# A decode kernel whose KV buffers also take the space set aside for GpSimd's transfer descriptors

## The chip, the core and the metric

The kernel runs on one core of one Trainium2 chip. The metric is the device time of one execution in microseconds. The core's engines are TensorE (PE; PEld is its weight load), VectorE (DVE), ScalarE (ACT), GpSimd (POOL) and SyncE (SP), which only issues transfers here. All weights and caches lie in the chip's memory (HBM) and come to on-chip memory (SBUF, 128 partitions) through 16 DMA engines; TensorE writes its results to PSUM, which has eight banks.

## The reference, cut to what matters

Two layers, each an attention block A and a feed-forward block B, with the same weights in both layers, for 4 tokens of 448 features, one new position each:

```
x = A_x                                   # 4 x 1 x 448
x = x + A(layernorm(x)); x = x + B(layernorm(x))
x = x + A(layernorm(x)); x = x + B(layernorm(x))

A(x): q = x @ wq                          # 448 -> 16 heads x 256
      k, v = the last 2048 positions of k_cache, v_cache   # 8 KV heads, two q heads share one
      p = softmax(q . k / 16);  o = p @ v;  return o @ wo  # 4096 -> 448
B(x): return (silu(x @ w_gate) * (x @ w_up)) @ w_down      # 448 -> 1792 -> 448
```

Everything is bf16. Each token has its own cache. One KV head of one token has 2048 x 256 values of K and as many of V: 1 MiB each. 4 tokens x 8 heads x 2 MiB are 64 MiB, and both layers read the same cache. So a layer that finds a K or V of the layer before still in SBUF needn't load it again.

## The kernel before, in words

**Units of work.** The work is cut into 64 heads (token, layer, KV head), written as three digits: 107 is token 1, layer 0, head 7; 113 is token 1, layer 1, head 3. PLAN (line 48) lists them in 54 groups of one head or two. For each head K and V come in two halves of 512 KiB. A buffer for one half is 128 x 2048 bf16; NPOOL = 27 of them lie in `kv`, and seven more (NWQ) hold wq until its last use, then seven late halves too.

**One group** (`group`, lines 916 to 1080) is a chain over the engines: two K transposes of 32 x 32 blocks on VectorE (L935), the masked query on GpSimd (L974), the scores on TensorE (`scores`, L969, 32 matmuls), row maxima on VectorE and TensorE (L982, L987, L990, L996), the exponential on ScalarE (L1000), a turn of the weights (L1013, L1022), sums (L1030, L1035), the V product (`pv`, L1044, 8 matmuls for each half of V), its reordering (L1059, L1061, L1067), division (L1057, L1077), and the output projection (`out_proj`, L1089 or L1097). PSUM has two banks for scores (S), three for products (Y), one that accumulates the output (A) and two for the projections and the FFN (Z, Z2).

Where the two halves of a K lie at most REACH = 15 buffers apart, `keys` (line 909) reads both with one matmul; else each score matmul becomes two of half the width.

**Between layers** each token has its own chain: residual, norm, FFN (`ffn_row`, or `ffn` for late tokens), norm, and the projection of the next query (`qproj`, lines 637 to 699). Only after it can the token's layer 1 start. Layer 0 of the next tokens is interleaved with it, so the order of the whole is: token 0 layer 0; token 1 layer 0 beside token 0 layer 1; and so on to token 3 layer 1. The first projection does all four tokens at once and needs all of wq.

**Kept heads.** KEEP_K and KEEP_V give, for each token, how many of its last heads of layer 0 keep their K or V in the buffers for layer 1. Before it is 5+5+4+5 = 19 K and 5+5+5+3 = 18 V, 37 MiB in all. A K that is kept is transposed once only. A buffer becomes free at the scores (K) or at the V product (V) of its last use.

**The order is written out.** Each engine runs its operations in the order of a list (SEQ_PE, SEQ_DVE, SEQ_ACT, SEQ_POOL, SEQ_SP), by the numbers in which `build` creates them. SEQ_SP is the order in which SyncE issues loads, and SLOTS gives the buffer for each. `schedule` adds to each load the wait for the operation that frees its buffer. SyncE issues in order: a load that waits holds up all behind it. In the lists "w" and "q" on TensorE are fills: matmuls with zero weights that add nothing to A (L1191, one matmul of 128 x 512; L1197, four of 32 x 512). `_fill` orders them against the operations of other engines that read or write A, by start times of `schedule`'s own estimate.

**Where things lie.** Tiles are allocated one after the other (lines 383 to 434). The first 16 KiB of each partition are kept by the language for descriptors of transfers that GpSimd issues (DynamicDMAScratch). This kernel issues its transfers from SyncE, and one small one from ScalarE.

Of the kernel before, what the change touches and what calls it, by code (L numbers as in the profile page):

```python
# [8 lines left out]
BF16 = mybir.dt.bfloat16  # L9
# [4 lines left out]
B = 4  # L14
# [11 lines left out]
NPOOL = 27  # L26
# [4 lines left out]
KEEP_K = (5, 5, 4, 5)  # L31
KEEP_V = (5, 5, 5, 3)
# [53 lines left out]
).split()  # L86
SEQ_DVE = (
# [23 lines left out]
).split()  # L111
# [1156 lines left out]
```

## Time and profile before

| what | us |
|---|---|
| median of 3 runs (lowest, highest) | 294.4 (293.93, 295.44) |
| span of the profiled execution, first to last instruction | 291.7 |
| busy: PE, DVE, POOL, ACT | 221.3, 197.4, 86.5, 66.1 |
| mean granted TensorE clock | 0.815 of full |
| bytes moved | 108.28 MB, 371 GB/s over the span |

The span is that of one execution with the profiler on; the runs' time includes what lies before and after it. The chain that ended last, followed back from the end, is 36% PE, 31% DMA, 12% waits of SyncE's queue and 12% DVE. "Place" means, below, the MB that stand ahead of a load in SEQ_SP: it is counted from the list (512 KiB for a half, 1 MiB for a piece of wq, 0.46 MB for a piece of wo, and so on), and is the same in any run.

### The profile page before, as it was taken

Reading aid. Unit: us, or ns where it says so; the run is one execution under the profiler, and the core shown is the slowest. Engines: PE = TensorE matmul, PEld = TensorE weight load, DVE = VectorE, ACT = ScalarE, POOL = GpSimd, SP = SyncE. Lnnn points to the kernel's source line nnn. Section 1 sums busy time; section 2 is a strip of 40 time slices with the busy share of each in tenths; the row PEclk is TensorE's granted clock in tenths of the full one; section 3 lists DMA queues with packets and bytes.
Section 4 is the critical chain, followed back from the end, with each engine's and each line's share of the span. In section 5 each row is a group of like instructions: output and inputs, shape, how many; then the busy total and the mean of one; then the engine's idle time right before and its main releaser. Section 6 shows DMA issues by size and latency. Waiting matters only on the chain.

```text
span 291.7 us, 10739 instructions
## 1 busy us (share of the span) xinstructions
PE 221.3 (76%) x4684; PEld 129.5 (44%) x4684; DVE 197.4 (68%) x609; ACT 66.1 (23%) x191; POOL 86.5 (30%) x230
## 2 busy tenths in 40 slices
PE   0467569686977697869688787797798667899775
PEld 0313136233433454546335454566364435645455
DVE  7547584427665997974968769677838777848541
ACT  0030002022214232322323233312312322033310
POOL 1541003111322233324323523340221331433522
PEclk9997977957689777886959559857759998799997
DMA  7999999999999999999999999999989999999800
GB/s 284 413 404 407 424 407 409 401 404 406 391 408 407 389 408 408 394 383 358 412 395 356 409 408 407 407 406 379 369 317 372 403 410 388 367 374 401 354 6 3
DMA packets 30782, 108.28 MB, mean 371 GB/s; under 512 B 3083, under 2 KB 7183, under 8 KB 29327
## 3 DMA queue, kind: packets, MB, share of 16 engines
q1 hardware_dynamic: 30727, 107.60, 94.3%
q8 instruction: 37, 0.61, 0.8%
q14 instruction: 10, 0.08, 0.1%
q10 hardware_dynamic: 8, 0.00, 0.0%
HBM read 107.58 MB, written 0.00 MB: 369 GB/s over the span
## 4 chain that ended last, share of the span: by engine, by line
PE 36%; DMA 31%; SPq 12%; DVE 12%; issue 5%; ACT 1%; POOL 1%
DMA half<-in_A_k_cache_dram 16%; DMA half<-in_A_v_cache_dram 15%; PE Y L1044 8%; PE S L969 8%; DVE half L935 7%; SPq L945 5%; SPq L550 5%; PE Z L773 3%; PE Z L665 2%; PE A L1097 2%; SPq L931 2%; PE Y L1013 2%; PE Z L813 2%; DVE oh L1061 1%; PE Y L1067 1%
## 5 line engine op out<-in xcount | busy, mean ns | idle before, releaser
L935 DVE STREAM_TRANSPOSE half<-half 128x1024 uint32<-128x1024 uint32 x90 | 110.0, 1232 | 14.9 <-DMA half<-in_A_k_cache_dram 14.4
L1044 PE MATMUL Y<-half,pT 128*4 128x256 bf16 (+1 forms) x1024 | 53.4, 319 | 11.8 <-DMA half<-in_A_v_cache_dram 8.8
L969 PE MATMUL S<-half,qe 128*8 128x128 bf16 (+1 forms) x1728 | 48.3, 261 | 10.6 <-DVE half L935 5.3
L1057 POOL TENSOR_TENSOR small<-small 128x2 f32<-128x2 f32 (+1 forms) x54 | 40.7, 758 | 51.6 <-DVE small L1035 44.9
L969 PEld LDWEIGHTS S<-half,qe 128*8 128x8 bf16 x1728 | 33.7, 95 | 19.3 <-DVE half L935 8.2
L974 POOL TENSOR_TENSOR qe<-qc,tiny 128x64 bf16<-128x64 bf16 x64 | 18.2, 292 | 79.9 <-PE S L969 66.3
L1000 ACT ACTIVATE praw<-S,small 104x128 bf16<-104x128 f32 (+1 forms) x54 | 20.8, 385 | 75.2 <-DVE small L996 65.7
L1061 DVE SCALAR_TENSOR_TENSOR oh<-oh,small,Y 128x256 bf16<-128x256 bf16 x54 | 25.3, 468 | 10.9 <-ACT oh L1059 10.4
L1059 ACT ACTIVATE oh<-Y 128x256 bf16<-128x256 f32 x54 | 20.6, 382 | 47.1 <-PE Y L1044 32.2
L1044 PEld LDWEIGHTS Y<-half,pT 128*4 128x4 bf16 (+1 forms) x1024 | 19.4, 88 | 24.0 <-DMA half<-in_A_v_cache_dram 12.0
L982 DVE TENSOR_REDUCE tiny<-S 104x1 bf16<-104x128 f32 (+1 forms) x54 | 16.4, 306 | 11.7 <-PE S L969 11.4
L1022 ACT ACTIVATE pT<-Y 128x64 bf16<-128x64 f32 (+1 forms) x54 | 13.1, 242 | 44.0 <-PE Y L1013 36.7
L1097 PE MATMUL A<-wo_sb,oT 128*4 128x448 bf16 x168 | 17.1, 399 | 3.7 <-DVE oT L1077 2.2
L1191 PE MATMUL A<-identb,small 128*128 128x512 bf16 x54 | 19.4, 444 | 0.0
L996 DVE TENSOR_REDUCE small<-S 104x1 f32<-104x32 f32 x54 | 9.6, 181 | 10.8 <-PE S L990 6.8
L665 PE MATMUL Z<-half,xn 128*5 128x512 bf16 x160 | 15.1, 530 | 1.6 <-DVE st L601 1.3
L1035 DVE TENSOR_REDUCE small<-Y 128x2 f32<-128x32 f32 (+1 forms) x54 | 10.0, 186 | 9.2 <-PE Y L1030 8.2
L987 PE MATMUL S<-small,identb 104*104 104x32 bf16 x54 | 12.5, 234 | 4.3 <-DVE tiny L982 3.3
L1077 DVE TENSOR_TENSOR oT<-Y,small 128x4 bf16<-128x4 f32 (+1 forms) x62 | 9.1, 157 | 7.8 <-PE Y L1067 4.4
L990 PE MATMUL S<-identb,tiny 104*104 104x32 bf16 x54 | 11.6, 219 | 3.6 <-issue 3.6
L1013 PE MATMUL Y<-sel,praw 104*64 104x32 bf16 x176 | 11.4, 206 | 3.7 <-ACT praw L1000 2.4
L1067 PE MATMUL Y<-tiny,oh 128*128 128x2 bf16 (+1 forms) x108 | 10.9, 171 | 3.8 <-DVE oh L1061 3.4
(142 smaller groups left out, 252.2 us busy)
## 6 DMA issues: line engine op xcount, KB each, us to landing
half<-in_A_v_cache_dram SPq DMA_DIRECT2D x92, 512.0 KB, 7.8
half<-in_A_k_cache_dram SPq DMA_DIRECT2D x74, 512.0 KB, 7.7
half<-in_A_k_cache_dram SPq DMA_DIRECT2D x8, 1024.0 KB, 16.4
wo_sb<-in_A_wo_dram SPq DMA_DIRECT2D x8, 448.0 KB, 14.9
half<-in_A_wq_dram SPq DMA_DIRECT2D x3, 1024.0 KB, 6.5
wd_sb<-in_B_w_down_dram SPq DMA_DIRECT2D x1, 1568.0 KB, 20.4
wg_sb<-in_B_w_gate_dram SPq DMA_DIRECT2D x1, 1344.0 KB, 16.8
wu_sb<-in_B_w_up_dram SPq DMA_DIRECT2D x1, 1344.0 KB, 17.3
```

What stands on the lines that cost most here:

```text
L665: last = e.matmul(zb[32 * j:32 * j + B + 1, 0:512], lhsT=lhsT, rhs=wq_sb[:, c:c + 512], start=(cc == 0), stop=(cc == 3), skip_group_check= ...
L935: return e.transpose(a, a)
L969: last = e.matmul(Sb[s_][qd:qd + 8, c0:c0 + rhs.free_size()], lhsT=qe[q_][:, P, ce, :, :].rearrange("p a n -> p (a n)"), rhs=rhs, start=(c ...
L974: g.op(POOL, 0.25, pos - SLEAD - 1, lambda e, P=P, t=t, kvh=kvh: e.tensor_tensor(qe[q_][:, P, :, :, :], qc[t][:, kvh, :, :].unsqueeze(2).b ...
L1000: return e.activation(praw[0:R, 0:128 * n].rearrange("p (g r l) -> p g r l", g=2 * n, l=2), Sb[s_][0:R, 0:128 * n].rearrange("p (l g r) -> ...
L1013: last = e.matmul(Yb[p_][64 * h:64 * h + 64, c0:c0 + (48 if n == 2 else 32)], lhsT=praw[0:R, 64 * gg:64 * gg + 64], rhs=w, start=(gg == 0) ...
L1044: last = e.matmul(Yb[p_][32 * gg:32 * gg + M, 256:512], lhsT=pT[pt][:, gg, 2 * a + hv, 4 * P:4 * P + M] if n == 2 else p1[:, gg % 2, 2 * a ...
L1057: g.op(POOL, 0.69, pos, lambda e: e.tensor_tensor(ri[p_][:, 0:2 * n], rs[p_][:, 0:2 * n], expo[:, 1:1 + 2 * n], op=ALU.pow), r=(f"rs{p_}", ...
L1059: g.op(SCA, 0.34, pos, lambda e: e.activation(oh[:, :], Yb[p_][:, 256:512], ACT.Copy), r=(f"y{p_}",), w=("oh",), bank=(f"Y{p_}",))
L1061: g.op(DVE, 0.43, pos, lambda e: e.scalar_tensor_tensor(out=oh[:, :], in0=oh[:, :], scalar=lomask[:, 0:1], in1=Yb[p_][:, 256:512], op0=ALU ...
L1097: last = e.matmul(Ab[32 * k:32 * k + B, 0:D], lhsT=oT[oi][:, k % 2, k // 2, :], rhs=wo_sb[:, 4 * kvh + k, :], start=False, stop=False, ski ...
L1191: return e.matmul(Ab[:, 0:512], lhsT=zero[:, 0:1].broadcast_to([128, 128]), rhs=identb[:, :].unsqueeze(1).broadcast_to([128, 4, 128]), sta ...
```

## The change

1. **Space.** The area for GpSimd's descriptors is cut from 16 KiB to 128 bytes of each partition (SCRATCH), and the rest takes w_down (12.25 KiB of each partition) and seven small tiles (selt, xs, wide, praw, one pT, oh) at fixed addresses. `fold` shrinks to a quarter, and the product that used it becomes four matmuls on 32 columns each.
2. **Buffers.** 31 halves instead of 27, beside the seven of wq.
3. **Kept heads.** 6+6+5+5 = 22 K and 6+6+6+4 = 22 V: 44 MiB instead of 37. Loads of layer 1: 14 halves fewer; six K transposes fewer.
4. **Orders.** SEQ_PE, SEQ_DVE, SEQ_ACT, SEQ_POOL, SEQ_SP and SLOTS are new. PLAN, and so the order in which groups are numbered, is the same. Merged loads (two halves with one instruction) are written in the list with "+": 6 instead of 8.
5. **Fills.** 105 "w" instead of 54 "w" and 20 "q". Their place against the operations on A is now written out (HELD), not taken from estimated times.

```diff
-NPOOL = 27
+SCRATCH = 128
+NPOOL = 31
-KEEP_K = (5, 5, 4, 5)
-KEEP_V = (5, 5, 5, 3)
+KEEP_K = (6, 6, 5, 5)
+KEEP_V = (6, 6, 6, 4)
...
-FILLD = 0.43
+FILLD = 0.22
...
     def schedule(self, npool):
+        pairs = [[self.ops[int(y)] for y in x.split("+")] for x in SEQ_SP if "+" in x]
+        order = {e: [self.ops[int(y)] for x in s if x[0] not in "wq" for y in x.split("+")] for e, s in seq.items()}
...
     def _fill(self):
-        held = sorted((o for o in self.ops if o.eng != PE and "A" in o.bank), key=lambda o: o.start)
+        held = [o for o in self.ops if o.eng != PE and "A" in o.bank]
+        after = dict(zip(held, map(int, HELD)))
...
+        for h in held:
+            if after[h]:
+                h.deps[fills[after[h] - 1]] = True
...
+        nc.dynamic_dma_scratch_size = SCRATCH
+        for a in nc.allocations() if callable(nc.allocations) else nc.allocations:
+            if a.name.startswith("DynamicDMAScratch"):
+                a.memorylocations[0].dims = [128, SCRATCH]
+        low = [SCRATCH]
+
+        def at(name, shape, dt):
+            t = nc.alloc_sbuf_tensor_at(name, shape, dt, offset=low[0])
+            size = {BF16: 2, FP32: 4}[dt]
+            for n_ in shape[1:]:
+                size *= n_
+            low[0] += -(-size // 32) * 32
+            assert low[0] <= 16384
+            return t
+
+        wd_sb = at("wd_sb", [128, NFC, D], BF16)
...
-        fold = sb("fold", [128, 4, 32], BF16)
+        fold = sb("fold", [128, 1, 32], BF16)
...
-        g.op(DVE, 0.2, R0, lambda e: e.tensor_copy(
-            fold[:, 1:4, :], fold[:, 0:1, :].broadcast_to([128, 3, 32])), r=("fold",), w=("fold",))
...
-            g.op(PE, 0.3, rank, lambda e: e.matmul(
-                Z2[:, 0:128 * n], lhsT=fold[:, :, :].rearrange("p q m -> p (q m)"), rhs=qS[:, 0:128 * n], start=True,
-                stop=True, skip_group_check=True), r=("wa", "fold"), w=("z2",), bank=("Z2",))
+            def spread_q(e):
+                for j in range(4):
+                    last = e.matmul(Z2[32 * j:32 * j + 32, 0:128 * n], lhsT=fold[:, 0, :], rhs=qS[:, 0:128 * n], start=True,
+                                    stop=True, skip_group_check=True)
+                return last
+            g.op(PE, 0.3, rank, spread_q, r=("wa", "fold"), w=("z2",), bank=("Z2",))
```

The numbers in the lists change with every operation that goes, so the lists can't be compared by eye. Counted out, they place the loads that matter here as follows (MB ahead of the load; for "last V" and wq the MB up to and with it):

| load | before | after |
|---|---|---|
| wq complete | 3.7 | 16.8 |
| first load into a buffer that was used | 21.5 | 23.6 |
| last V of token 0, layer 0 | 24.6 | 28.1 |
| first load that waits for work behind token 0's next projection | 38.9 (scores of 013) | 35.8 (V product of 100, which now stands behind the projection's transposes) |
| last V of token 1, layer 0 | 49.9 | 48.9 |
| first load that waits for scores of 116 | 62.5 | 58.8 |
| last V of token 2, layer 0 | 71.9 | 71.4 |
| first load that waits for scores of 213 | 84.5 | 80.8 |
| last V of token 3, layer 0 | 93.9 | 88.7 |
| first load into wq's buffers | 103.4 | 95.5 |
| all loads | 107.6 | 100.2 |

The halves of five K lie more than 15 buffers apart in the new SLOTS (007, 104, 103, 107 and 202; the first four are kept, so nine groups read them); none did before.

More of the change, by code (lines that the diff above doesn't have):

```diff
@@ L60 @@
 SEQ_PE = (
[25 rows of a table removed]
[25 rows of a table added]
 ).split()
 SEQ_DVE = (
[23 rows of a table removed]
[22 rows of a table added]
 ).split()
 SEQ_ACT = (
[8 rows of a table removed]
[8 rows of a table added]
 ).split()
 SEQ_POOL = (
[9 rows of a table removed]
[9 rows of a table added]
 ).split()
 SEQ_SP = (
[9 rows of a table removed]
[8 rows of a table added]
 ).split()
 SLOTS = (
[5 rows of a table removed]
[5 rows of a table added]
+).split()
+HELD = (
+    "0 29 29 35 42 42 42 48 48 55 61 61 61 61 65 65 71 73 78 91 91 91 91 93 93 93 93 95 95 95 95 95 95 102 102"
 ).split()
@@ L247, in schedule @@
     def schedule(self, npool):
-        self.real = len(self.ops)
         seq = {PE: SEQ_PE, DVE: SEQ_DVE, SCA: SEQ_ACT, POOL: SEQ_POOL, SP: SEQ_SP}
-        order = {e: [self.ops[int(x)] for x in s if x[0] not in "wq"] for e, s in seq.items()}
+        pairs = [[self.ops[int(y)] for y in x.split("+")] for x in SEQ_SP if "+" in x]
+        order = {e: [self.ops[int(y)] for x in s if x[0] not in "wq" for y in x.split("+")] for e, s in seq.items()}
         assert sum(map(len, order.values())) == len(self.ops) == len({o for s in order.values() for o in s})
@@ L253, in schedule @@
         last = {id(c): o for o in self.ops for c in o.rel}
-        held, slot, second = [None] * npool, dict(zip(loads, map(int, SLOTS))), {}
-        for a, b in list(zip(order[SP], order[SP][1:]))[:44]:
-            if a not in second and a.both and b.both and (a.cell if a.mate is None else a.mate) is (b.cell if b.mate is None else b.mate) and abs(slot[a] - slot[b]) == 1:
-                second[b] = a
+        held, slot, second = [None] * npool, dict(zip(loads, map(int, SLOTS))), {b: a for a, b in pairs}
+        for a, b in pairs:
+            assert (b.mate is a.cell or a.mate is b.cell) and abs(slot[a] - slot[b]) == 1
         for o, s in slot.items():
@@ L270, in schedule @@
         order[SP] = [o for o in order[SP] if o not in second]
+        self.order = order
         self.ops = [o for o in self.ops if o not in second]
@@ L274, in schedule @@
             o.succ = [d for d in o.deps]
+        self._fill()
+        for o in self.ops:
+            o.succ = list(o.deps)
         free, at = {e: 0.0 for e in order}, {e: 0 for e in order}
@@ L296, in schedule @@
                 n += 1
-        self.order = order
         self.span = max(o.end for o in self.ops)
-        self._fill()
         self._place_waits()
     def _fill(self):
-        held = sorted((o for o in self.ops if o.eng != PE and "A" in o.bank), key=lambda o: o.start)
-        out, fills, t, real = [], [], 0.0, iter(self.order[PE])
+        held = [o for o in self.ops if o.eng != PE and "A" in o.bank]
+        after = dict(zip(held, map(int, HELD)))
+        assert len(held) == len(HELD)
+        out, fills, real = [], [], iter(self.order[PE])
         for x in SEQ_PE:
-            if x[0] not in "wq":
-                o = next(real)
-                t = o.end
-            else:
+            if x[0] in "wq":
                 o = Op(len(self.ops), PE, FILLD, 0, self.filler(x[0] == "w"))
-                o.start, o.end = t, t + 0.01
-                for d in {h.eng: h for h in held if h.start < t}.values():
-                    o.deps[d] = True
+                for e in (DVE, SCA, POOL):
+                    ahead = [h for h in self.order[e] if after.get(h, len(fills) + 1) <= len(fills)]
+                    if ahead:
+                        o.deps[ahead[-1]] = True
                 self.ops.append(o)
                 fills.append(o)
-                t = o.end
-            o.pos = len(out)
-            out.append(o)
+            out.append(o if x[0] in "wq" else next(real))
         for h in held:
-            before = [f for f in fills if f.start <= h.start]
-            if before:
-                h.deps[before[-1]] = True
+            if after[h]:
+                h.deps[fills[after[h] - 1]] = True
         self.order[PE] = out
@@ L388, in build @@
         wu_sb = sb("wu_sb", [128, 3 * FF + FF // 2], BF16)
-        wd_sb = sb("wd_sb", [128, NFC, D], BF16)
         kv = sb("half", [128, (NPOOL + NWQ) * HALF], BF16)
@@ L398, in build @@
         pmax = [tiny[:, 24 + s:25 + s] for s in range(NS)]
-        selt = [sb(f"selt{h}", [128, 4, 12], BF16) for h in range(2)]
+        selt = [at(f"selt{h}", [128, 4, 12], BF16) for h in range(2)]
         sel1 = [sb(f"sel1{h}", [128, 4, 2, 2, 2], BF16) for h in range(2)]
@@ L415, in build @@
         xio_k = ("wo7",)
-        xsc = sb("xs", [128, 4, B], FP32)
+        xsc = at("xs", [128, 4, B], FP32)
         xs = xsc[:, :, :].rearrange("p c t -> p t c")
@@ L422, in build @@
         colsum = qc[0][:, :, :, :].rearrange("p k c h -> p (k c h)").bitcast(FP32)[:, 0:2 * NFC].rearrange("p (g f) -> p g f", g=2)
-        wide = sb("wide", [128, 512], FP32)
+        wide = at("wide", [128, 512], FP32)
         wideb = wide[:, :].bitcast(BF16)
@@ L430, in build @@
         xf = xfc.rearrange("p (c t) -> p t c", t=B)
-        praw = sb("praw", [128, 256], BF16)
-        pT = [sb(f"pT{s}", [128, 4, 4, 12], BF16) for s in range(NP)]
-        oh = sb("oh", [128, DH], BF16)
+        praw = at("praw", [128, 256], BF16)
+        pT = [(at, sb)[s](f"pT{s}", [128, 4, 4, 12], BF16) for s in range(NP)]
+        oh = at("oh", [128, DH], BF16)
         oT = [sb(f"oT{s}", [128, 2, 2, B], BF16) for s in range(2)]
```

156 rows, old and new, of tables (SEQ_ACT, SEQ_DVE, SEQ_PE, SEQ_POOL) are left out of this document.

## The prediction

> **What bounds the kernel now.** I read the slices of the page first, then the queues, then a table by stage, then TensorE in order of time. The slices (tenths of busy time, GB/s):
>
> ```profile
> DMA  7999999999999999999999999999989999999800
> GB/s 284 413 404 407 424 407 409 401 404 406 391 408 407 389 408 408 394 383 358 412 395 356 409 408 407 407 406 379 369 317 372 403 410 388 367 374 401 354 6 3
> ...
> q1 hardware_dynamic: 30727, 107.60, 94.3%
> q8 instruction: 37, 0.61, 0.8%
> q14 instruction: 10, 0.08, 0.1%
> q10 hardware_dynamic: 8, 0.00, 0.0%
> ```
>
> The transfers run at some 400 GB/s from the second slice to the 38th: they are the bound, except in a few dips and in the last two slices. All 107.6 MB go through q1, which SyncE feeds. The stages (busy us of PE, PEld, DVE, ACT, POOL; granted clock, DMA share, GB/s):
>
> ```profile
> 0.00:5.00 5.00, 0.00 (x0) 0.00 (x0) 3.70 (x35) 0.00 (x0) 0.83 (x9) 1.00 0.61 218
> ...
> 2.00:125.00 123.00, 87.70 (x1546) 45.14 (x1546) 81.54 (x242) 23.39 (x66) 31.58 (x84) 0.82 1.02 404
> 125.00:163.00 38.00, 29.74 (x615) 16.91 (x615) 28.57 (x90) 10.75 (x32) 13.65 (x37) 0.78 1.00 382
> 163.00:200.00 37.00, 29.80 (x729) 19.58 (x728) 27.34 (x78) 9.93 (x32) 12.01 (x30) 0.72 1.03 408
> 200.00:220.00 20.00, 18.08 (x391) 11.07 (x390) 13.01 (x38) 5.04 (x14) 4.46 (x12) 0.66 0.93 342
> ...
> 245.00:277.00 32.00, 28.72 (x703) 18.75 (x704) 21.90 (x72) 8.55 (x22) 11.67 (x28) 0.89 0.97 374
> ```
>
> Undisturbed flow is 404 GB/s. From 125 to 163 and from 200 to 220 it falls to 382 and 342: 38 x 22/404 = 2.1 us and 20 x 62/404 = 3.1 us are lost there, while TensorE is 78% and 90% busy. From 245 on TensorE is 90% busy and carries the end. The first stretch gives the start: 218 x 5 = 1.09 MB, 2.7 us at 404, so bytes flow from 2.3 us, 1.6 us after the first issue (0.72 in the timeline of SyncE). A load at place x MB in SyncE's list is thus through at 2.3 + x/0.404, plus what has been lost.
>
> TensorE in order of time, the rows that I use below (start, us):
>
> ```profile
> 16.55 1.45 PE L665 MATMUL Z<-half,xn 128*5 128x512 bf16 x12 [1.32 <-DVE st L601]
> ...
> 24.07 1.02 PE L969 MATMUL S<-half,qe 128*8 128x128 bf16 x32 [1.26 <-POOL qe L974]
> ...
> 66.46 1.02 PE L1044 MATMUL Y<-half,pT 128*4 128x256 bf16 x16 [0.28 <-DVE small L1035]
> ...
> 90.41 0.26 PE L681 MATMUL Z<-identb,wide 128*128 128x4 bf16 x4
> ...
> 127.72 0.39 PE L1044 MATMUL Y<-half,pT 128*4 128x256 bf16 x8
> ...
> 155.33 0.66 PE L969 MATMUL S<-half,qe 128*8 128x128 bf16 x32
> ...
> 185.86 0.39 PE L1044 MATMUL Y<-half,pT 128*4 128x256 bf16 x8
> ...
> 212.88 1.02 PE L969 MATMUL S<-half,qe 128*8 128x128 bf16 x32
> ...
> 243.02 0.39 PE L1044 MATMUL Y<-half,pT 128*4 128x256 bf16 x8 [0.81 <-DMA half<-in_A_v_cache_dram]
> ```
>
> They are, from the third on: the last V product of token 0's first layer; the last piece of the projection that follows it; the last V product of token 1 and the first scores of its second layer; the same pair for token 2; the last V product of token 3.
>
> **The change, part by part.**
>
> *Fewer bytes.* KEEP_K and KEEP_V sum to 44 heads where they summed to 37. Seven loads of 1 MiB go: 7.34 MB, 18.2 us at 404 GB/s. Six transposes go with them (L935, 1232 ns each): 7.4 us of VectorE beside the loads, worth nothing by themselves. 18.2 us is the most that the change can give unless it also loses less in the dips.
>
> Here the Trainium skill speaks against counting so. DMA: Bandwidth & Descriptors, Specifications, puts HBM at about 358 GB/s for a core; by that the 100.2 MB that are left would need 280 us, and the end would come near 300. The rows disagree: 404 over 123 us, and 107.6 MB within some 275 us. I give that no chance.
>
> *A later first projection.* The last piece of wq stands at place 16.8 MB (before: all of it by 3.7), so it lands at 2.3 + 16.8/0.404 = 44 us. The 32 matmuls and what follows took 24.07 - 16.55 = 7.5 us, so the first scores come at about 51 us, not 24. The loads need no freed buffer before place 23.6 MB (60.7 us), so nothing stalls by this alone; but attention has 27 us less to reach the next point.
>
> *Tighter layer boundaries.* When a token's last head of layer 0 is done, its FFN, its norms and its next projection run one after the other, and only then are the buffers of its kept heads read and freed. What counts is the room, in MB, between that last head's V and the first load that must wait for the far side, against the time C of that chain. The loads stall for about 0.5 (the V product) + C + 1.6 (a start) - room.
>
> - Token 0: room 35.8 - 28.1 = 7.7 MB, 19.1 us. (Before, the load behind the far side was at 38.9 and the last V at 24.6: 35 us.) C is 67.5 to 90.7 = 23.2 us, because the V product that frees the buffer is now queued behind the projection's last transposes. In the new lists three K transposes instead of six stand in VectorE's part of the chain, 3.7 us less: 19.5 to 23.2. Stall 2.5 to 6.2; I take 4, about the middle.
> - Token 1: room 58.8 - 48.9 = 9.9 MB, 24.5 us (before 62.5 - 49.9, 31 us). C is 128.1 to 156.0 = 27.9; without one group of scores (0.7 to 1.0) and with V there earlier (TensorE waited 0.5 and 0.9 us for it) 25.7. Stall 3.3 to 5.5; I take 4.
> - Token 2: room 80.8 - 71.4 = 9.4 MB, 23.3 us (before 31). C is 186.2 to 213.9 = 27.7; five transposes (6.2 us) fewer stand in it: 21.5 to 27.7. Stall 0.3 to 6.5; I take 3.
>
> For before the same sum gives no stall at the three, yet the dips cost 5.2 us, so the small losses around a boundary come on top: 2 us taken, 0 to 8 as bounds (before: its last V product of token 3 ends at 243.4 where 2.3 + 93.9/0.404 + 0.5 = 235.2, so 8.2 us had been lost in all).
>
> *The last stage.* From the last V product of token 3 to the end of the span are 291.7 - 243.4 = 48.3 us, with TensorE 90% busy; the remaining 13.7 MB need only 34 of it, now 11.5 MB and 28. So fewer bytes don't shorten this stage; it only starts earlier. Its chain loses four fills (80 quarter fills, 417 ns each, four to a fill): about 1 us. 47.3 taken, 46 to 48.3.
>
> *Small parts.* 105 full fills of 444 ns (L1191) instead of 54, and 20 in quarters: about 20 us more busy TensorE, 27 of them before the first scores, where it idles, the rest put where it waits for another engine. Inside the three chains there are 27 instead of 8; if each were in the way, 19 x 0.44 = 8.4 us; if they keep the clock up (0.66 in 200 to 220), a group of scores takes 0.66 instead of 1.02 us, over 8 groups 3 us back. I take nothing, since they stand before waits. Five K pairs lie over 15 slots apart, in nine groups: 32 more score matmuls each, between 0 and 1.02 us (a group's own time), 0 to 9 us, spread over the whole run and mostly beside loads: nothing, nearest to the row that doubles the width without more time. The fold is applied by four small matmuls instead of one, five times (L693 259 ns; the four of L739 together 0.26): nothing. One setup copy (0.2 us) goes. Six merged loads instead of eight: beside the flow. New addresses of w_down and small tiles: no row depends on an address; nothing, by L813's 1.6 us per use at most a few tenths.
>
> **The sum.** Last V of token 3 at place 88.7: 2.3 + 219.6 + 0.5 = 222.4; stalls 4 + 4 + 3 = 11; small losses 2; last stage 47.3: a span of 282.7 us. The profiled execution's span is 291.7 and the median of the three runs 294.4; the 2.7 us between are added: 285.4, forecast **285 us**, 3.2% faster.
>
> **Rivals.**
>
> *The bytes alone decide* (0.22). The new order hides the boundaries as the old one did, and all 18.2 us come: 276.2. For it: the 408 GB/s from 163 to 200 with TensorE at 81%, and fills where TensorE would idle. Against it: three rooms shorter by 7 to 16 us than before.
>
> *The late projection is never made up* (0.08), slower. From the first scores to the V product that must free the load at 35.8 MB, before took 24.1 to 86.8 = 62.7 us. If that repeats from 51 on, the load goes out at 113.7 and flows at 115.3, where the flow was dry at 90.9: 24.4 us lost, 294.4 - 18.2 + 24.4 = 300.6. It decides from a stretch of 57 us on. Against it: in that stretch of before TensorE was busy about 45 us, some 20 of them fills, and waited for V; without those waits 40 us should do.
>
> *The room isn't free* (0.02): something moves descriptors through that memory and the tiles collide or get no space; then about 294, as before. The queue rows show no GpSimd queue, and the issues on the page are SyncE's and one of ScalarE. The Trainium skill, SBUF — State Buffer, SBUF size, says that 16 KiB of each partition are set aside for the descriptors of GpSimd's software queues; by that a kernel with no such transfer leaves them idle, and the rows agree.
>
> **How the numbers follow.** Forecast and neighbourhood 0.68 (279 to 291.5), then 0.22, 0.08, 0.02. The bounds of the terms give 222.4 + 6.1 + 0 + 46 + 2.7 = 277 to 222.4 + 18.2 + 8 + 48.3 + 2.7 = 299.6; the range reaches down to the first rival and leaves the top, which needs every term at its worst: 275.5 to 292.5. About 0.5% (1.5 us) is what a measurement of this kernel can tell from no change: faster than 292.9 0.87, between 0.05, slower 0.08.
>
> **What would show it.** L935 x84, L1191 x105, L969 x2016, 100.2 MB: the change does what it says. First scores near 51 us with the flow still at 400. Dips near 90, 150 and 205 to 212 us of a few us each: the boundaries; none: the first rival. A dip of over 18 us near 90: the second. From token 3's last V product to the end 46 to 48 us; much less would say that the last stage, too, was held by the loads.

## The result and the profile after

The change makes the kernel slower: a median of 323.1 us (322.7 to 323.3) against 294.35 us before, a ratio of 1.098 (95%: 1.092 to 1.103). The forecast was 285. The profiled execution's span is 321.5 us, against 291.7. Here and below a time is the median of all runs of a kernel, while a ratio with its 95% interval uses only the runs within 1.5% of that kernel's fastest, so the two can differ by as much.

The slices of the changed kernel's page (tenths of busy time, GB/s), and its main queue:

```profile
DMA  7999999999905995597989797799999989969400
GB/s 271 405 412 415 401 411 405 404 406 391 388 34 222 370 414 222 209 335 237 345 315 331 296 383 295 297 346 345 369 370 353 363 331 384 334 210 361 174 0 5
...
q1 hardware_dynamic: 28999, 100.26, 81.9%
```

A slice is 8.0 us. Up to 88 us the row is that of before. Then come a nearly dry slice (34 GB/s) and a half dry one (222), and after one slice of 414 the flow stays between 209 and 384 GB/s up to 297 us, where before showed some 400 with a few dips. So fewer bytes take longer. The same by stage, cut at the last V products and the first scores of the tokens (busy us of PE, PEld, DVE, ACT, POOL; granted clock, DMA share, GB/s):

```profile
52.30:81.00 28.70, 21.31 (x580) 13.44 (x581) 13.80 (x45) 7.16 (x24) 8.70 (x19) 0.87 1.04 401
81.00:102.80 21.80, 17.86 (x221) 7.36 (x217) 10.45 (x35) 4.35 (x10) 5.00 (x15) 0.66 0.51 197
102.80:149.30 46.50, 37.70 (x962) 23.11 (x962) 29.65 (x76) 10.02 (x34) 12.60 (x33) 0.69 0.80 304
149.30:173.70 24.40, 21.06 (x367) 10.51 (x371) 16.22 (x52) 6.86 (x19) 8.00 (x22) 0.76 0.91 325
173.70:218.00 44.30, 34.89 (x827) 20.09 (x827) 31.06 (x82) 10.41 (x33) 12.96 (x33) 0.78 0.86 322
218.00:241.10 23.10, 18.10 (x443) 11.29 (x444) 13.89 (x52) 5.97 (x19) 7.18 (x19) 1.00 0.97 362
241.10:269.00 27.90, 22.96 (x493) 12.88 (x493) 19.01 (x54) 7.13 (x22) 9.98 (x25) 0.82 0.94 358
269.00:321.50 52.50, 43.38 (x995) 28.14 (x995) 29.14 (x103) 11.14 (x28) 14.98 (x36) 0.82 0.53 195
```

81.0, 149.3, 218.0 and 269.0 are the ends of the last V products of layer 0 of tokens 0 to 3 (before: 67.5, 128.1, 186.2, 243.4). 102.8, 173.7 and 241.1 are the first scores of the next layer 1. So lines 2, 4 and 6 are the boundaries, the chains between two layers; lines 3, 5 and 7 are the stages in between, in which layer 1 of one token and layer 0 of the next are interleaved. The reader is to see that the boundaries have the expected length (22 to 24 us), and that the flow is low in the stages between them too. The same three stages in before:

```profile
94.00:128.10 34.10, 27.56 (x716) 16.87 (x716) 29.74 (x74) 10.16 (x34) 11.23 (x30) 0.80 1.02 396
...
155.30:186.20 30.90, 24.51 (x621) 15.27 (x613) 25.89 (x70) 9.06 (x29) 12.04 (x30) 0.78 1.02 399
...
212.90:243.40 30.50, 23.26 (x568) 13.85 (x571) 21.27 (x61) 8.00 (x25) 9.43 (x23) 0.91 0.98 379
```

The lengths alone don't compare, since the new order puts more of TensorE's work into the first two (962 and 827 matmuls, before 716 and 621; 160 and 96 of them come from the K pairs that lie far apart). The flow does: 304 and 322 GB/s, before 396 and 399. The chain that ended last tells the first stage from the others: in before, 63% of it from 94 to 128.1 us is transfers of K and V; in the changed kernel hardly any from 102.8 to 149.3, where VectorE waits 0.4 us for a K and TensorE for no V, but 47% from 173.7 to 218 and 32% from 241.1 to 269.

What SyncE's queue waits for, in the changed kernel (us in total, times, longest):

```profile
SPq L945 <- PE Y L1060: 49.3, 16, 7.8
SPq L961 <- PE S L985: 30.1, 8, 5.9
...
SPq L961 <- PE S L1006: 19.4, 5, 15.2
```

L945 issues K loads and L961 V loads; L1060 is the V product, L985 the scores, and L1006 a matmul of the row maxima right behind the scores: loads wait for buffers to be freed. Such waits alone prove little, since before has them too (31.4 us for K behind the V product, 49.3 here): a queue that issues ahead always waits for the next buffer. What counts is whether the transfers run dry meanwhile.

### The profile page after: what moved, and what is told of

It reads as the page before. It is cut to its first block, busy times and chain, and to the rows that moved or that the text cites. A ratio compares the mean times of both kernels' runs of the same rounds, so it can differ in the third digit from the quotient of the medians.

```text
span 321.5 us, 11250 instructions
## 1 busy us (share of the span) xinstructions
PE 233.6 (73%) x4958; PEld 132.3 (41%) x4958; DVE 192.4 (60%) x602; ACT 65.7 (20%) x191; POOL 87.5 (27%) x230
## 2 busy tenths in 40 slices
DMA packets 29056, 100.98 MB, mean 314 GB/s; under 512 B 2891, under 2 KB 6991, under 8 KB 27855
## 3 DMA queue, kind: packets, MB, share of 16 engines
q1 hardware_dynamic: 28999, 100.26, 81.9%
## 4 chain that ended last, share of the span: by engine, by line
PE 52%; DMA 15%; DVE 12%; SPq 9%; issue 6%; ACT 4%; POOL 0%
PE Y L1060 11%; PE S L985 11%; PE A L1207 8%; DMA half<-in_A_v_cache_dram 7%; DVE half L951 5%; SPq L563 5%; DMA half<-in_A_k_cache_dram 4%; DMA half<-in_A_wq_dram 4%; PE Z L678 3%; PE A L1113 3%; PE Y L1029 3%; PE Z L789 2%; SPq L947 2%; PE S L1003 2%; PE Z L739 1%
## 5 line engine op out<-in xcount | busy, mean ns | idle before, releaser
L951 DVE STREAM_TRANSPOSE half<-half 128x1024 uint32<-128x1024 uint32 x84 | 102.7, 1233 | 18.1 <-DMA half<-in_A_k_cache_dram 17.7
L985 PE MATMUL S<-half,qe 128*8 128x128 bf16 (+2 forms) x2016 | 47.6, 247 | 16.5 <-issue 9.9
L1060 PE MATMUL Y<-half,pT 128*4 128x256 bf16 (+1 forms) x1024 | 50.2, 314 | 8.0 <-DMA half<-in_A_v_cache_dram 3.3
L1073 POOL TENSOR_TENSOR small<-small 128x2 f32<-128x2 f32 (+1 forms) x54 | 40.9, 759 | 53.7 <-DVE small L1051 38.8
L985 PEld LDWEIGHTS S<-half,qe 128*8 128x8 bf16 x2016 | 34.6, 94 | 30.0 <-issue 11.5
L1207 PE MATMUL A<-identb,small 128*128 128x512 bf16 x105 | 44.4, 527 | 1.4 <-DVE xr L880 0.7
L678 PE MATMUL Z<-half,xn 128*5 128x512 bf16 x160 | 14.2, 507 | 26.8 <-DMA half<-in_A_wq_dram 26.6
L1077 DVE SCALAR_TENSOR_TENSOR oh<-oh,small,Y 128x256 bf16<-128x256 bf16 x54 | 25.4, 471 | 13.7 <-ACT oh L1075 12.9
L998 DVE TENSOR_REDUCE tiny<-S 104x1 bf16<-104x128 f32 (+1 forms) x54 | 16.8, 312 | 26.6 <-PE S L985 26.2
L1060 PEld LDWEIGHTS Y<-half,pT 128*4 128x4 bf16 (+1 forms) x1024 | 20.9, 90 | 21.6 <-issue 6.0
L1113 PE MATMUL A<-wo_sb,oT 128*4 128x448 bf16 x168 | 16.2, 399 | 2.7 <-DVE oT L1093 2.7
L678 PEld LDWEIGHTS Z<-half,xn 128*5 128x5 bf16 x160 | 3.9, 99 | 32.6 <-DMA half<-in_A_wq_dram 27.1
L1051 DVE TENSOR_REDUCE small<-Y 128x2 f32<-128x32 f32 (+1 forms) x54 | 10.1, 191 | 11.4 <-PE Y L1046 8.5
L1012 DVE TENSOR_REDUCE small<-S 104x1 f32<-104x32 f32 x54 | 9.8, 181 | 10.9 <-PE S L1006 10.4
L1207 PEld LDWEIGHTS A<-identb,small 128*128 128x128 bf16 x105 | 10.4, 122 | 10.4 <-issue 7.0
L1029 PE MATMUL Y<-sel,praw 104*64 104x32 bf16 x176 | 11.4, 203 | 3.6 <-ACT praw L1016 2.7
L1083 PE MATMUL Y<-tiny,oh 128*128 128x2 bf16 (+1 forms) x108 | 10.9, 170 | 3.0 <-DVE oh L1077 2.7
## 6 DMA issues: line engine op xcount, KB each, us to landing
wd_sb<-in_B_w_down_dram SPq DMA_DIRECT2D x1, 1568.0 KB, 18.4
```

What stands on the lines that cost most here:

```text
L678: last = e.matmul(zb[32 * j:32 * j + B + 1, 0:512], lhsT=lhsT, rhs=wq_sb[:, c:c + 512], start=(cc == 0), stop=(cc == 3), skip_group_check= ...
L951: return e.transpose(a, a)
L985: last = e.matmul(Sb[s_][qd:qd + 8, c0:c0 + rhs.free_size()], lhsT=qe[q_][:, P, ce, :, :].rearrange("p a n -> p (a n)"), rhs=rhs, start=(c ...
L1029: last = e.matmul(Yb[p_][64 * h:64 * h + 64, c0:c0 + (48 if n == 2 else 32)], lhsT=praw[0:R, 64 * gg:64 * gg + 64], rhs=w, start=(gg == 0) ...
L1060: last = e.matmul(Yb[p_][32 * gg:32 * gg + M, 256:512], lhsT=pT[pt][:, gg, 2 * a + hv, 4 * P:4 * P + M] if n == 2 else p1[:, gg % 2, 2 * a ...
L1073: g.op(POOL, 0.69, pos, lambda e: e.tensor_tensor(ri[p_][:, 0:2 * n], rs[p_][:, 0:2 * n], expo[:, 1:1 + 2 * n], op=ALU.pow), r=(f"rs{p_}", ...
```

## The theories

The first two came straight from the profile: **A**, the late first projection holds everything up; **C**, the fills behind the first scores are in the way. Against both stood **B**, that the new orders as a whole cost it, so that the old order with the new space and the 44 kept heads gains what was forecast.

As stated, all three missed in the first four runs (below). What the slow kernels had in common was the space and the number of kept heads, and that gave the next theories: **P**, the new addresses or the cut descriptor area slow something; **R**, too few buffers are left beside the kept heads; **W** (later **E**), the engines need their time for a stage whatever is loaded (as E: once the buffers are enough).

## The experiments

Each was timed in three rounds against the kernel before on the same chip. A short diff stands with each; "old order" is the lists of before, without the loads and transposes that the kept heads make needless, and with buffers chosen anew: each load takes the one that comes free first.

**e1, projection first.** In the changed kernel wq, then heads 001 and 000, are loaded first; on VectorE the projection's copies go ahead of the K transposes.

```diff
 SEQ_SP = (
-    "48 149+151 236+238 118 369 367 50 308 146 209+211 127 125 51 259 123 186+188 155+157 128 307 232 120 240 52 233 "
+    "48 49 50 52 51 155+157 123 125 127 128 159 160 149+151 236+238 118 369 367 308 146 209+211 259 186+188 307 232 "
```

> The changed kernel with one thing moved: wq is loaded first, then K and V of heads 001 and 000, and VectorE does the first projection's copies ahead of the K transposes; buffers, kept heads, and all later orders stay. Theory A (late start): from the first scores to the end the changed kernel took 321.5 - 52.3 = 269.2 us, before 291.7 - 24.1 = 267.6; the work is paced from the first scores on, so scores at about 27 us give a span near 296 and a time of 296 to 300. Theory B (late buffers): the loads starve in every stage because the new lists leave too little room between the work that frees a buffer and the load that takes it; only the first gap (about 9 us near 90 us) goes, 311 to 316. Theory C (fills in the way): no more than the first gap either, 311 to 321.

Measured: 324.0 us, 1.099 (1.089 to 1.108). The first scores came at 34.3 instead of 52.3 us, but token 0's last V product ended at 83.7 instead of 81.0, though by the trace its V landed at 73.5 us, as in the changed kernel (73.7). All three ranges lay below. The edit removes the late scores and not the late end of token 0, whose cause stays open; it refutes only that the start of the scores costs the 29 us.

**e2, before with wq late.** In the kernel before, one piece of wq is loaded at place 16.4 MB instead of 1.0.

```diff
 SEQ_SP = (
-    "50 49 51 53 52 124 126 184 183 154 155 147 233 210 212 285 287 234 128 129 150 152 156 158 187 189 308 237 239 "
-    "160 161 214 215 266 267 121 119 262 264 191 309 192 289 290 260 241 242 393 395 118 368 370 120 122 416 418 "
+    "49 51 53 52 124 126 184 183 154 155 147 233 210 212 285 287 234 128 129 150 152 156 158 187 189 308 237 239 "
+    "160 50 161 214 215 266 267 121 119 262 264 191 309 192 289 290 260 241 242 393 395 118 368 370 120 122 416 418 "
```

> The kernel before, with the first piece of wq (1 MiB) moved from place 1.0 MB to place 16.4 MB in the list of loads; nothing else. Theory A: first scores near 52 instead of 24 us and the whole end 25 to 30 us later, 318 to 324. Theory B: the old lists have room, so most of the late start is made up: 295 to 303. Theory C says nothing of it.

Measured: 315.9 us, 1.061 (1.048 to 1.075), between the ranges of A and B. In the old order a late projection does cost some 18 us.

**e3, no late fills.** The changed kernel without the 78 fills behind the first scores; fills add nothing to the output.

```diff
-    "130 165 132 w 135 193 216 195 168 137 218 w 139 140 198 170 243 268 245 200 144 172 173 270 202 147 221 174 175 "
+    "163 130 165 132 135 193 216 195 168 137 218 139 140 198 170 243 268 245 200 144 172 173 270 202 147 221 174 "
...
```

> The changed kernel without the 78 fills that come after the first scores; the 27 ahead of them stay. Theory C: the fills take 78 x 0.53 = 41 us of TensorE behind the first scores, and half of them or more stand in the chains: 295 to 308. Theories A and B: fills stand where TensorE waits; 316 to 323, or some us slower if the granted clock falls.

Measured: 321.4 us, 1.085 (1.074 to 1.095). C falls.

**e4, old order, 44 kept.** The changed kernel's space, 31 buffers and 44 kept heads, with the old order.

```diff
 KEEP_K = (6, 6, 5, 5)
 KEEP_V = (6, 6, 6, 4)
 SEQ_PE = (
-    "53 w w w w w w w 57 w w w 60 w w w 68 w 71 w w w 79 w w 82 w 90 w 93 w w w 106 107 103 104 109 110 112 w w w 163 "
+    "53 57 60 68 71 79 w 82 90 w w 103 93 104 106 107 109 w 110 112 130 w 132 w w w w 135 w 137 w w w w w w w w 139 "
...
```

> The space of the change (31 buffers, w_down and small tiles in the descriptors' place) and its 44 kept heads, but with the lists of the kernel before, from which the 14 loads and six transposes that fall away are struck out; each load takes the buffer that is free earliest. Theory A: first scores at 24 us and 268 us of paced work behind them, so the 7 MB bring next to nothing: 288 to 294. Theory B: the old lists with 7 MB less and more buffers have at least the old rooms, so the bytes count: 276 to 283.

Measured: 325.4 us, 1.098 (1.087 to 1.109), far above both ranges. This was the turn: scores began at 24.4 us and token 0 ended at 66.8, as before, and yet the kernel was as slow as the changed one. Its two stages with the largest loss:

```profile
94.40:145.00 50.60, 34.13 (x718) 20.85 (x717) 28.46 (x72) 10.36 (x34) 11.31 (x29) 0.57 0.71 257
...
172.60:216.90 44.30, 29.15 (x617) 17.63 (x609) 26.23 (x70) 9.14 (x29) 11.90 (x30) 0.62 0.76 269
```

257 and 269 GB/s, with TensorE busy for two thirds only. Its matmuls wait for V and VectorE waits for K (us in total, times, longest):

```profile
PE Y L1062 <- DMA half<-in_A_v_cache_dram: 19.9, 17, 4.1
```

```profile
DVE half L953 <- DMA half<-in_A_k_cache_dram: 37.8, 23, 4.8
```

The engines wait for loads while the loads wait for the engines: a ring with too few buffers in it.

**A count of the buffers.** For each load the trace gives the issue, the end of its first use (the scores for K, the V product for V) and the end of the operation that frees its buffer. Between issue and first use I call a buffer working, from then until it is freed kept. Means over the interleaved stages of tokens 1, 2 and 3, with the time from issue to first use ("hold") of the loads issued there, and the flow from the stage table:

| kernel | buffers | kept | working | hold, us | GB/s |
|---|---|---|---|---|---|
| before | 27 | 15.7, 15.7, 14.9 | 11.1, 11.2, 10.6 | 12.6, 13.3, 13.5 | 396, 399, 379 |
| changed | 31 | 22.2, 22.5, 18.8 | 8.7, 8.3, 12.0 | 13.4, 12.2, 17.2 | 304, 322, 358 |
| e4 | 31 | 23.5, 23.6, 19.4 | 7.2, 7.3, 11.2 | 13.3, 12.9, 14.7 | 257, 269, 367 |
| e5 | 31 | 15.7, 15.7, 14.9 | 14.7, 14.5, 15.7 | 16.6, 17.2, 19.8 | 408, 399, 407 |

The flow is about working buffers x 0.524 MB / hold, and at most the transfers' own 404 to 410. For the changed kernel's first stage that is 8.7 x 0.524 / 13.4 = 340 GB/s (304 measured), for e4's 7.2 x 0.524 / 13.3 = 284 (257), for before's 462, where the transfers are the lower. The hold includes the time for which a landed load waits for its engine, so the count by itself doesn't say which of the two is late; the runs that follow change the number of buffers. Four buffers more and six to seven halves more in use as kept ones (in the first two stages): that is the trade. At the narrowest place, 20 of 27 and 24 of 31, both leave 7, which is what hides it.

**e5, space only.** e4 with the 37 kept heads of before.

```diff
-KEEP_K = (6, 6, 5, 5)
-KEEP_V = (6, 6, 6, 4)
+KEEP_K = (5, 5, 4, 5)
+KEEP_V = (5, 5, 5, 3)
```

> The changed kernel's space and its 31 buffers, but the 37 kept heads and the order of the kernel before (only the buffer numbers are new). Theory R (too few buffers are left for the loads in transit: 31 less 24 kept halves is 7, as 27 less 20 was, but the kept ones are held longer, 21 on average from 90 to 290 us in the old order with 44 heads against 15 before): now 11 are left at the narrowest place, so it is no slower than before, and some of the 8 to 11 us of its dips come back: 283 to 293. Theory P (the new addresses, or the descriptor area of 128 bytes, slow something): about 30 us slower than before, as with 44 heads in the same order: 315 to 325. Theory W (the engines need some 57 us for a stage whatever is loaded): as before, 292 to 296.

Measured: 289.1 us, 0.989 (0.985 to 0.994): 1.1% faster than before and far faster than the changed kernel. P and W fall, R holds. Its slices:

```profile
DMA  7999999999999999999999999999999999999200
GB/s 278 417 399 410 423 408 409 404 400 409 388 409 410 408 408 408 407 407 405 410 405 371 405 412 408 408 407 407 405 409 404 408 408 407 402 401 404 111 5 3
```

Between the first slice and the last three only two fall below 399 GB/s (388 and 371): with 11 buffers at the narrowest place nearly all of the 107.6 MB flow at 399 to 423. So the new addresses and the small descriptor area cost nothing that shows.

**e6 and e7, some of the seven heads.** e5 with one K and one V more of token 2 and one V more of token 3 (e6), or with one K and one V more of tokens 0 and 1 (e7).

```diff
-KEEP_K = (5, 5, 4, 5)
-KEEP_V = (5, 5, 5, 3)
+KEEP_K = (5, 5, 5, 5)
+KEEP_V = (5, 5, 6, 4)
```

```diff
-KEEP_K = (5, 5, 4, 5)
-KEEP_V = (5, 5, 5, 3)
+KEEP_K = (6, 6, 4, 5)
+KEEP_V = (6, 6, 5, 3)
```

> As the one with the space alone, but 40 kept heads: one K and one V more of token 2, one V more of token 3 (3 MiB fewer to load, 7.8 us at 404 GB/s). At the narrowest place 9 buffers are left instead of 11. R: the stages of tokens 0 and 1 as with the space alone, token 2's somewhat slower: 280 to 295. P: 307 to 320. W: 292 to 296.

> As the one with the space alone, but 41 kept heads: one K and one V more of tokens 0 and 1 (4 MiB fewer to load, 10.4 us). 7 buffers are left while token 0's or token 1's 24 halves are held. R: the two stages after their last heads of layer 0 take 78 and 72 us as with 44 heads in the old order, not 61 and 58: 310 to 322. P: 305 to 320. W: 292 to 296.

Measured: e6 290.1 us, 0.988 (0.983 to 0.993): 3 MiB fewer, no gain over e5. e7 308.7 us, 1.060 (1.052 to 1.069): a little better than R said (310 to 322). In e7 the stage from token 0's to token 1's last V product took 77.8 us, as in e4 (78.2) and not as in e5 (61.6); the next two took 58.1 and 54.1, near e5's 55.4 and 55.2. The price is paid where the heads are kept. The second slow stage that R expected, from token 1's to token 2's, did not come: in its interleaved part 19.9 halves were kept and 10.9 worked, against 23.6 and 7.3 in e4.

**e8, 34 buffers, 44 kept.** e4 with three buffers more, for which w_up is left out.

```diff
-NPOOL = 31
+NPOOL = 34
-        wu_sb = sb("wu_sb", [128, 3 * FF + FF // 2], BF16)
+        wu_sb = wg_sb
```

> The old order with 44 kept heads, but 34 buffers. Their space comes from leaving out w_up: its tile is that of w_gate, used twice, and its load is 16 KB instead of 1.6 MB (3.9 us less to load at 404 GB/s). The work of the engines is unchanged. R: with 10 buffers left at the narrowest place the flow is back at 380 to 404 GB/s, and 98.7 MB take 22 us less than before: 270 to 285. P: as with 31 buffers less 4: 313 to 325. W: 290 to 296.

Measured: 286.3 us, 0.983 (0.972 to 0.995). Three buffers give back 39 us; the 1.6 MB of w_up are some 4 of them at 404 GB/s. The two stages of e4 in e8, where 10.5 and 10.0 buffers work:

```profile
92.70:126.30 33.60, 27.67 (x716) 17.76 (x714) 27.89 (x72) 10.05 (x34) 11.27 (x30) 0.80 0.99 368
...
149.20:182.80 33.60, 28.17 (x619) 17.77 (x611) 25.91 (x70) 9.13 (x29) 11.93 (x30) 0.61 0.97 359
```

But R had said 270 to 285: the missing 22 us of loads brought 7 to 8 against before, and 3 against e5.

**e9 and e10, 37 buffers.** w_down is left out too; 44 kept heads (e9) or 37 (e10).

```diff
-NPOOL = 34
+NPOOL = 37
-        wd_sb = at("wd_sb", [128, NFC, D], BF16)
+        wd_sb = wg_sb[:, :].rearrange("p (c n) -> p c n", n=D)
```

> As the kernel with 34 buffers (old order, 44 kept heads), but 37 buffers: w_down is left out too, its tile is that of w_gate again, and its load is 8 KB. 13 buffers are left at the narrowest place, and 97.1 MB are loaded. Theory R alone (the buffers left for loads in transit set the flow): the flow stays near 404 GB/s, loads end 26 us earlier than with the space alone (10.5 MB less than 107.6), and the end comes at 262 to 270. Theory E (with enough buffers the engines need 55 to 60 us for each token's stage, as in the runs with 37 kept and 31 buffers and with 44 kept and 34: 55.2 to 61.6): 282 to 287, as with 34 buffers.

> Control for the one with 37 buffers and 44 kept heads: the same, with the 37 kept heads of the kernel before, 104.4 MB. 17 buffers are left at the narrowest place. R: the flow was already at 404 to 410 GB/s with the space alone, so only the 3.2 MB that are left out count, 7.9 us: 279 to 283. E: 282 to 289.

Measured: 285.9 us, 0.968 (0.960 to 0.977), and 286.0 us, 0.970 (0.963 to 0.977). With buffers enough, 7 MB fewer bytes are worth 0.1 us, and transfers are only 10% and 6% of the chain that ended last (31% before). E holds in the old order: from one token's last V product to the next one's e9 takes 62.3, 52.1 and 57.0 us (in an execution 2.8 us longer than its median) and e10 60.0, 50.9 and 57.1.

**e11, before with 24 buffers.** The kernel before, in its own space.

```diff
-NPOOL = 27
+NPOOL = 24
```

> The kernel before, in its own space, order and kept heads, with 24 instead of 27 buffers: 4 left at the narrowest place. R: in the two stages between first scores of the second layer and the last V product, 8 and 6 buffers work instead of 11 and 9, as in the old order with 44 heads, where these stages took 51 and 44 us instead of 34 and 31: 315 to 345. E, or a theory in which the number of kept heads itself costs time: 293 to 300.

Measured: 347.9 us (342.6 to 349.0) against 294.3 in the same batch, above the range of R but for the lowest run, and far from E. In the three interleaved stages 8.0, 8.2 and 8.9 buffers work, at 303, 316 and 328 GB/s; the first:

```profile
98.30:146.30 48.00, 34.12 (x718) 20.76 (x717) 30.51 (x74) 10.25 (x34) 11.27 (x29) 0.57 0.86 303
```

So the shortage needs neither the new space nor the additional kept heads; taking three buffers away is enough.

**e12, e13, e15 and e16, the new orders with more buffers.** The changed kernel's own lists with 34 buffers (e12) and 37 (e15), as in e8 and e9; e13 and e16 are these two with the lists of e1.

```diff
-NPOOL = 31
+NPOOL = 34
```

> The changed kernel with its own new orders, fills and 44 kept heads, but 34 buffers (buffer numbers new; w_up left out as in the other kernel with 34 buffers, 3.9 us less to load). R: the stages come back to 55 to 60 us. If the late first projection then costs as much as in the kernel before with wq late (20 us), 300 to 308; if the new orders make up for it, 282 to 290. If the buffers are not the cause in the new orders: 315 to 323.

> The new orders with 44 kept heads and 34 buffers (w_up left out), and wq, then K and V of heads 001 and 000, loaded first, the projection's copies ahead of the K transposes. With 31 buffers this edit was worth nothing. Theory L (the 17 us between the new orders and the old one at 34 buffers, 303.6 and 286.3, are the late first projection): 284 to 292. Theory O (they lie in the rest of the new orders, above all the 44 us from token 2's first to last V product of layer 0, against 34 in the old order): 296 to 304.

> The changed kernel's own orders, fills and 44 kept heads with 37 buffers (w_up and w_down left out, 7.1 us less to load than with 31). The old order needed no more than 34: 286.3 with 34, 285.9 with 37. Theory R (the new orders are short of buffers even with 34, so that the rest of the 17 us goes as well): 284 to 293. Theory O (the new orders themselves cost it, whatever the buffers): 298 to 305.

> The same with 37 buffers and the first projection early (wq, then heads 001 and 000, loaded first). With 31 and 34 buffers the early projection was worth nothing. R with the late projection as what is left: 284 to 290, and less than the run beside it. O: as the run beside it, 298 to 308.

Measured: e12 303.6 us, 1.029 (1.019 to 1.039); e13 309.2 us, 1.045 (1.033 to 1.056); e15 299.9 us, 1.020 (1.012 to 1.027); e16 304.4 us, 1.022 (1.012 to 1.032). e13 lies above both of its ranges. Three buffers thus give the new orders 20 us back, three more another 4, and the last 14 us against e9 lie in the orders (O holds). But two things went with the three buffers: w_up's 1.6 MB (some 4 us at 404 GB/s), and 288 score matmuls, because in the new SLOTS no K pair lies far apart (1728 instead of 2016). The scores keep TensorE busy for 47.6 us in the changed kernel, 46.6 in e12 and 43.0 in e15. So these two can be up to some 9 of the 20 us; no run took them apart.

Where the 14 us lie, e16 against e10 shows, 13.0 us apart at the end: token 0's last V product ends 12.0 us later (78.6, 66.6); the three stretches from token to token take 1.5 less, 11.4 more and 10.2 less (58.5, 62.3 and 46.9), and the end after token 3 1.3 more. So it is token 0's delay that stays. The early projection brings nothing, and it does not end token 0 earlier: 78.6 in e16, 77.0 in e15. In these two 27.8 MB lie ahead of token 0's last V, 24.4 in e10, which is 8.4 us at 404 GB/s; by the trace that V lands at 73.1 and 63.9 us.

**e14, no fills.** e10 without the 70 fills behind the first scores.

```diff
 SEQ_PE = (
-    "53 57 60 68 71 79 w 82 90 w w 103 93 104 106 107 109 w 110 112 130 w 132 w w w w 135 w 137 w w w w w w w w 139 "
+    "53 57 60 68 71 79 w 82 90 w w 103 93 104 106 107 109 w 110 112 130 132 135 137 139 140 144 147 163 193 165 195 "
...
```

> As the one with 37 buffers and 37 kept heads (w_up and w_down left out), without the 70 fills behind the first scores; they add nothing to the output. With enough buffers that kernel and the one with 44 kept heads both take 286 us, so the loads don't set the time there. Theory T (TensorE's own time sets it): the fills' 27 us are partly saved, 268 to 280. Theory C (the chain of each group and the chains between layers set it, and the fills stand in waits): 284 to 290; above that if the clock that is granted falls without them.

Measured: 284.6 us, 0.970 (0.962 to 0.977), against 286.0 with them. T's range is missed. The granted clock fell without the fills (e10, then e14, below), and the matmuls that are left took longer: 276 instead of 262 ns for the scores, 343 instead of 317 for the V product. So TensorE's busy time fell by 7.8 us only (220.0 to 212.2), though the fills had taken some 28, and the run does not exclude that TensorE's time counts. That the chains between the engines, C, set these 286 us is likely, and not shown. The granted clocks:

```profile
core 0: 282.8 us, clock 0.835
```

```profile
core 0: 283.3 us, clock 0.734
```

## Why the prediction was wrong

**What was right.** The counts (84 transposes, 105 fills, 2016 score matmuls, 100.26 MB). The first scores at 52.3 us (51). The chains at the boundaries: 21.8, 24.4 and 23.1 us, where the ranges or the value were 19.5 to 23.2, 25.7, and 21.5 to 27.7. That the space is free: transposes take 1231 ns in e5 and 1232 before, and the flow is 408 GB/s. The Trainium skill, SBUF — State Buffer, SBUF size, calls that area the reserve of the software descriptor rings; e5 agrees, which leaves 128 bytes of it and takes 289.1 us.

**The step that failed** is "the small losses around a boundary come on top: 2 us taken, 0 to 8 as bounds". What a stretch loses is its length x (404 - GB/s) / 404:

| | forecast, us | measured, us |
|---|---|---|
| boundaries of tokens 0, 1, 2 | 4 + 4 + 3 = 11 | 11.2 + 4.8 + 2.4 = 18.4 |
| all the rest up to token 3's last V | 2 | 11.5 + 9.0 + 3.2 = 23.7 |
| transfers that are already past that V's place | 0 | 4.5 |
| last stage | 47.3 | 52.5 |

The 4.5 is what is left of 269.0 - 222.4; by the stage table 90.0 to 90.7 MB had been moved at 269.0 (52.5 x 0.195 off the 100.26 MB of q1, or off all 100.98), 1.3 to 2.0 past the place of 88.7, which is 3.3 to 5.0 us. 7.4 + 21.7 + 4.5 + 5.2 = 38.8 us, the whole distance from the forecast span of 282.7 to 321.5.

The largest term is the middle one: the interleaved stages. I took the flow of before there (396 and 399 GB/s) as a property of the transfers and carried it over: "through at 2.3 + x/0.404, plus what has been lost". It was a property of some 11 working buffers, and the change leaves 8.7 and 8.3 in the first two stages. The bounds 0 to 8 came from before, so they could not hold what only the change makes. I counted only rooms, in MB, at three boundaries, and not, for each place, the buffers less the kept halves, which the lists give. That the number of buffers decides is shown in the old order: with 44 heads, 31 buffers give 257 and 269 GB/s in these stages, 34 give 368 and 359 (e4, e8); with 37 heads, 24 give 303 and 316, 27 give 396 and 399 (e11, before). In the changed kernel itself the first of these stages waits hardly for loads, with TensorE busy for 37.7 of 46.5 us; how much of its 11.5 us is the shortage, and how much the pace of the engines there, stays open.

A smaller step failed at token 0's boundary, which lost 11.2 us where the bounds were 2.5 to 6.2, though its chain of 21.8 was as forecast. "0.5 (the V product)" lets that product follow its load at once; the load landed at 73.7 us, and the product ended at 81.0. Why TensorE was so far behind is not shown; with the scores 18 us earlier (e1) it was 10 us behind.

**The gain was not there to be had, either.** "18.2 us is the most that the change can give" took the loads for the only bound. With buffers enough, and w_up and w_down left out, the old order with 7 MB fewer is 0.1 us faster (e9, e10): behind the loads, only 8 us away, stands a bound that is not the loads'. What an order written for 44 heads and enough buffers would reach was not tried.

**The rivals.** "The bytes alone decide" falls with the result, and with e9 and e10 even where buffers are enough. "The late projection is never made up" had the right side, at 0.08, by another way: its stall at place 35.8 MB was priced at 24.4 us, and the boundary of token 0 lost 11.2. What is left of it is that token 0 ends 10 to 12 us late, which is not made up, with buffers enough too; but in e16 it does so with an early projection. "The room isn't free" falls with e5.

**The sum of the 29 us.** From one series of runs to the next, each beside 293.4 to 295.5 us before: 294.3 before; 285.9 with buffers enough and 44 heads in the old order (-8.4); 299.9 with the new orders (+14.0); 303.6 with 34 buffers (+3.7); 323.1 with 31 (+19.5). So the shortage of buffers costs up to 23 us in the new orders (up to 39 in the old one: 325.4 and 286.3) and the orders 14. In these steps w_up and w_down are left out as well, 3.2 MB or 7.9 us at 404 GB/s (some 4 us of the 39), and in the new orders the 288 score matmuls; the chips differ from series to series. Which entries of the lists cost the 14, beyond the 3.4 MB more ahead of token 0's last V, stays open; no run changed them one at a time. Nor was it tried what a shorter hold would do with 44 heads and 31 buffers.

## What to carry to other kernels

A tile that is kept to save a load takes a buffer from the loads in transit for as long as it is kept. Before keeping more, count for each stage, not only for the narrowest place, buffers less kept ones, times their size, over the time from issue to first use, and compare that with the bandwidth: here some 11 working halves of 0.5 MB, each held 13 us, were just enough (380 to 400 GB/s), and 7 to 9 cost a fifth to over a third of the flow. And ask what stands behind the transfers before counting saved bytes as saved time: here, in the old order, it was 8 us away.

The Trainium skill, Perfetto Trace Analysis, Optimization Strategy, says that the same gap, repeated on the engine that should be saturated, can mean too little space for the next tile; e4 agrees, where VectorE waits 37.8 us in 23 places for K and TensorE 19.9 us in 17 for V, and with three buffers more (e8) 9.6 us in 8 and 4.6 us in 6.

## What the hardware showed that I had not expected

The time is steep in the number of buffers and then flat: 325.4 us with 31, 286.3 with 34 and 285.9 with 37 (44 heads, old order), and 347.9 with 24, 294.3 with 27 and 289.1 with 31 (37 heads). And leaving out the fills came out even: the mean granted TensorE clock fell from 0.84 to 0.73 of full and the matmuls got longer, but the fills' own time went, and the run took 284.6 us instead of 286.0.
